# Block 3's down product and the last block's steps merged in one stage of a three-part kernel, with block 3's tokens turned by TensorE

## The chip, the cores and the metric

The kernel runs on one core of a Trainium2 chip. Its time is the device time of one launch in microseconds, the median of several launches. A profile is taken of one further execution. The engines are TensorE (PE; its weight loads are listed as PEld), VectorE (DVE), ScalarE (ACT), GpSimd (POOL) and SyncE (SP, which here only issues DMA transfers). Each executes its own queue in order.

## What is computed

Three layers, one behind the other, in fp32:

```python
q_p, k_p = phi(q * s), phi(k * s)               # 4 batches, 8 heads, 576 tokens, 128 features
x = (q_p @ (k_p.T @ v)) / (q_p @ k_p.sum(tokens) + 1e-6)      # linear attention -> 2304 x 512
gate = 1.0 / (1.0 + np.exp(-(x @ w_gate)))      # 512 -> 1536
x = gate * (x @ w_val) @ w_out                  # 1536 -> 512
logits = x @ phi                                # 512 -> 32 slots: 8 experts of 4
d = softmax(logits, over=tokens)
h = np.maximum((d.T @ x)[e] @ w1[e], 0.0)       # per expert e, 512 -> 1024
slot_out[e] = h @ w2[e]                         # 1024 -> 512
out = softmax(logits, over=slots) @ slot_out
```

## The kernel before

Tokens lie in five blocks: blocks 0 to 3 have 512 of them, the last one (block 4) has 256. In the gated layer a block goes through 12 steps, one for each 128 of the 1536 hidden features. A step has a gate product, a value product and a down product, which adds to four banks of PSUM. Every fp32 product is made of three passes: operands are split into a high part (`hi_of`, a copy that rounds) and the rest (`lo_of`, a subtraction), and `three` adds high x high, high x low and low x high. So a product of 128 features with one block has 12 matmuls (four groups of 128 rows, three passes each), of 512 columns, or of 256 for the last block.

Blocks 2 and 3 are a pair (`pair_jobs`). Their gate and value products are made together, by seven products instead of eight. Block 2's down product runs inside these steps; the hidden features of block 3 are kept in `GB` (fp32, in the region `g` and the pieces g1a and g1b), and block 3's down product follows as a stage of its own (`SPAND`, 33 us). Then come the last block's 12 steps (`moe_jobs`). Both load the same out weights, converted earlier and kept in DRAM (`wscr`, for each of the 12 f one gate, one value and one out part of 128x512), into the six slots of 128x512 of the ring `ws` (`WR`), and split them: for block 3 in `split_out`, for the last block in `split_w`.

The gate of a full block is a chain of Abs, Exp, Ln, a VectorE operation that reads the bank once more, and Exp. The last block's gate is one Sigmoid. Where a function follows on ScalarE that is in another set of tables than the one before it, its queue has an ACT_TABLE_LOAD ahead of it, which the compiler puts there.

When a block has left the gated layer (`evac_out`), the operations of the slot layer for its tokens follow (`moe2_chunks`): logits (`chunk_logits`), the running maximum and exp over tokens, tokens turned to token-major form, the turned exponentials (`chunk_ltT`, tile `lt`) times the turned tokens, added to `acc` (`chunk_slot`), and exp over slots (`cs`, `cT`). To turn the tokens of blocks 0 to 3, VectorE transposes 32x32 squares (`chunk_x2`, 4 operations of 128x512) and 16 DMA transfers of 64 KB on SP's queue (`chunk_back`, `x2T<-x`) bring the squares to their places. The last block's tokens are turned in `last_slots` by TensorE (product with `ident`) and two copies. `join_slots` brings `acc` to a common maximum. Then `last_slots`, `layer1` (8 experts, weights W1), `layer2` (weights W2) and `combine` end the program.

W1 (16.8 MB) is loaded by ScalarE's queue into regions of SBUF as they become free, W2 (32 pieces of 512 KB) by SP's queue into the regions that fall free towards the end (`free_more`, `free_halves`, `free_early`, `free_rest`).

The order on each engine isn't that of the code. Each job is given a due time (`jobs.append((time, stream, job))`), and each operation that it records is given to `Plan`, with a lead for its stream (`LEAD`). `Plan.schedule` then runs a model of the five engines with costs of its own (`cost`, `RELOAD` for a change of table) and puts the operations in an order for each engine; `Plan.issue` writes them out. So all instructions have one line of code, L425 (L432 in the changed kernel), and are told apart by their tiles: `ga`, `va`, `o0` to `o3`, `fl` (two buffers) are the eight banks of PSUM, written as `o` where numbers are left out; `w0`, `w1`, `w2` are the split weights of gate, value and out; `gt` the split hidden features, `XT4` the last block's input, `ga_a` the gate's scratch.

## Time and profile before

| | before |
|---|---|
| median of 3 runs | 669.89 us (667.93 to 673.65) |
| the profiled execution | 666.81 us, its span 664.9 us, mean granted clock 0.997 |
| busy: PE, DVE, ACT, POOL | 644.0, 479.7, 410.6, 289.2 us |
| block 3's down product | about 513.5 to 547 us of the span |
| the last block's 12 steps | about 547 to 611 us |
| last slots; layer 1; layer 2 | 611 to 618; 618 to 632.5; 632.5 to 655 us |

Times in the views are microseconds from the span's start. "Idle before" an instruction is the time its engine stood still ahead of it, with the engine and tile of the instruction that ended it (`[0.46 <-DVE w]`). Ends of matmuls are modelled, so a group's shown length is longer than the time from its start to the next one's start.

### The profile page before, as it was taken

Reading aid. Unit: us, or ns where it says so; the run is one execution under the profiler, and the core shown is the slowest. Engines: PE = TensorE matmul, PEld = TensorE weight load, DVE = VectorE, ACT = ScalarE, POOL = GpSimd, SP = SyncE. Lnnn points to the kernel's source line nnn. Section 1 sums busy time; section 2 is a strip of 40 time slices with the busy share of each in tenths; the row PEclk is TensorE's granted clock in tenths of the full one; section 3 lists DMA queues with packets and bytes.
Section 4 is the critical chain, followed back from the end, with each engine's and each line's share of the span. In section 5 each row is a group of like instructions: output and inputs, shape, how many; then the busy total and the mean of one; then the engine's idle time right before and its main releaser. Section 6 shows DMA issues by size and latency. Waiting matters only on the chain.

```text
span 664.9 us, 12634 instructions
## 1 busy us (share of the span) xinstructions
PE 644.0 (97%) x4268; PEld 513.2 (77%) x4268; DVE 479.7 (72%) x1379; ACT 410.6 (62%) x937; POOL 289.2 (43%) x272
## 2 busy tenths in 40 slices
PE   7899999999999999999999999999999999899995
PEld 5676777768888888888877778878888779899663
DVE  5898989888998765667689987557557757756323
ACT  4899989889998866777675654534442225445012
POOL 0456344455445344455453555555551453542100
PEclk9999999999999999999999999999999999999998
DMA  7987857678976345223315552222228899777988
GB/s 233 324 269 260 274 188 273 204 237 272 298 260 215 101 115 176 90 97 98 109 49 185 195 147 78 63 64 63 65 65 293 278 316 346 229 233 264 353 334 240
DMA packets 55216, 132.17 MB, mean 199 GB/s; under 512 B 6256, under 2 KB 14192, under 8 KB 55152
## 3 DMA queue, kind: packets, MB, share of 16 engines
q1 hardware_dynamic: 49328, 114.01, 52.7%
q10 hardware_dynamic: 5824, 17.37, 7.7%
q8 instruction: 33, 0.54, 0.3%
q14 instruction: 31, 0.25, 0.1%
HBM read 113.00 MB, written 14.16 MB: 191 GB/s over the span
## 4 chain that ended last, share of the span: by engine, by line
PE 84%; DMA 5%; DVE 4%; ACT 2%; POOL 1%; SPq 1%; issue 1%; DVEq 0%; POOLq 0%; ACTq 0%
PE o L425 24%; PE fl L425 23%; PE va L425 19%; PE ga L425 18%; DMA g<-in_tok 2%; DMA x2T<-x 1%; DMA g<-in_w 1%; DVE g L425 1%; DMA ws<-wscr 1%; SPq L425 1%; DVE XT L425 1%; POOL g L425 1%; DVE ga_a L425 1%; ACT w L425 0%; DMA g<-in_qkT 0%
## 5 line engine op out<-in xcount | busy, mean ns | idle before, releaser
L425 POOL TENSOR_TENSOR w<-ws,w 128x512 fp32r<-128x512 f32 (+1 forms) x101 | 120.6, 1195 | 161.3 <-ACT w L425 67.2
L425 PE MATMUL o<-gt,w 128*128 128x512 f32 (+1 forms) x576 | 134.7, 372 | 2.2 <-POOL w L425 0.9
L425 PEld LDWEIGHTS o<-gt,w 128*128 128x128 f32 x576 | 97.2, 189 | 24.4 <-issue 2.4
L425 PE MATMUL ga<-XT,w 128*128 128x512 f32 (+1 forms) x432 | 101.6, 367 | 0.9 <-POOL XT L425 0.9
L425 ACT ACTIVATE w<-ws 128x512 fp32r<-128x512 f32 (+1 forms) x100 | 57.7, 579 | 72.3 <-PE o L425 28.1
L425 PE MATMUL va<-XT,w 128*128 128x512 f32 (+1 forms) x432 | 100.1, 366 | 1.6 <-DVE ga_a L425 1.1
L425 PE MATMUL fl<-g,g 64*128 64x128 f32 (+4 forms) x686 | 84.1, 313 | 3.5 <-ACT g L425 1.7
L425 ACT ACTIVATE g<-g 128x128 f32<-128x128 f32 (+4 forms) x206 | 73.8, 414 | 16.9 <-DVE g L425 12.9
L425 PEld LDWEIGHTS ga<-XT,w 128*128 128x128 f32 x432 | 69.9, 189 | 16.8 <-issue 4.7
L425 PEld LDWEIGHTS va<-XT,w 128*128 128x128 f32 x432 | 70.5, 189 | 15.2 <-issue 2.4
L425 PEld LDWEIGHTS fl<-g,g 64*128 64x128 f32 (+2 forms) x686 | 60.3, 182 | 24.4 <-issue 7.3
L425 ACT ACTIVATE x2T<-g 128x512 f32<-128x512 f32 x72 | 45.8, 666 | 4.2 <-DVE x L425 2.4
L425 ACT ACTIVATE g1b<-g1b,g 128x128 f32<-128x128 f32 x128 | 40.8, 389 | 5.9 <-DVE g L425 5.7
L425 DVE TENSOR_SCALAR x2T<-x2T 128x512 f32<-128x512 f32 (+1 forms) x72 | 35.9, 513 | 3.7 <-ACT x2T L425 3.4
L425 POOL TENSOR_TENSOR g<-g 128x640 f32<-128x640 f32 (+1 forms) x19 | 23.4, 1230 | 33.3 <-DMA g<-in_tok 13.3
L425 DVE CUSTOM_DVE_ANT_0 g<-fl,g 128x128 f32<-128x128 f32 x142 | 32.3, 286 | 6.5 <-PE fl L425 6.4
L425 PE MATMUL o<-gt,ga_a 128*128 128x512 f32 x144 | 35.4, 393 | 0.0
L425 DVE TENSOR_TENSOR XT<-fl,XT 128x512 f32<-128x512 f32 x24 | 16.6, 690 | 23.0 <-PE fl L425 23.0
L425 POOL TENSOR_TENSOR x<-x2T 128x512 int32<-128x512 int32 x19 | 24.6, 1295 | 16.1 <-DVE x2T L425 11.3
L425 PEld LDWEIGHTS o<-gt,ga_a 128*128 128x128 f32 x144 | 26.7, 188 | 5.8 <-POOL ga_a L425 0.3
L425 ACT ACTIVATE ga_a<-ga_a 128x512 f32<-128x512 f32 x48 | 30.0, 624 | 1.7 <-DVE ga_a L425 1.4
L425 POOL TENSOR_TENSOR w<-x,w 128x512 fp32r<-128x512 f32 x15 | 19.3, 1285 | 24.2 <-DVE x2T L425 11.5
(254 smaller groups left out, 1264.3 us busy)
## 6 DMA issues: line engine op xcount, KB each, us to landing
ws<-wscr SPq DMA_DIRECT2D x42, 512.0 KB, 3.7
g<-in_wall SPq DMA_DIRECT2D x36, 512.0 KB, 5.0
ws<-wscr SPq DMA_DIRECT2D x54, 256.0 KB, 3.7
wscr<-x SPq DMA_DIRECT2D x36, 256.0 KB, 4.6
g<-in_qkT SPq DMA_DIRECT2D x15, 576.0 KB, 5.3
g<-in_tok SPq DMA_DIRECT2D x15, 576.0 KB, 5.1
g<-in_w ACTq DMA_DIRECT2D x16, 512.0 KB, 6.9
XT<-in_w ACTq DMA_DIRECT2D x12, 512.0 KB, 4.6
```

The source lines that it names most:

```text
L425: ins = getattr(self.eng[e], method)(*a, **k)
```

## The change

Block 3's down product and the last block's 12 steps are put into one stage, `tail_jobs`. In step f the out part is loaded and split once (`split_t(f, 2)`), and both blocks use it: `down_b` (block 3, 512 columns, banks ga, va, o0, o1) in step f and `down_c` (last block, 256 columns, banks o3 and fl) one step later. The last block's value and gate products share one bank, `o2`: the value in columns 256 to 511, the gate in 0 to 255. The ring has five slots; the sixth is the gate's scratch. The gates of f = 10 and 11 use Abs, Exp, Ln and Exp, with a `preload` of the table set that has Exp and Ln, and their value goes to bank ga. Block 3's tokens are turned by 16 TensorE products with `ident` and four copies (`turn_block`) in place of 4 VectorE transposes and 16 transfers. Its slot layer and the join fall at the end, from the last `down_b` on. W1's loads have other times (`W1S`), two pieces of the last expert's W1 are loaded in `last_slots`, and the regions for W2 fall free in another order.

```diff
     def load_part(k):
+
         if todo:
             m = todo.pop(0)
-            slot[USE[m]] = k
-            W[USE[m]] = WR[:, k, :]
-            SP.dma_start(out=W[USE[m]], in_=wscr[USE[m][0] % NF][:, USE[m][1], :])
+            f, p = USE[m]
+            slot[f, p] = k
+            SP.dma_start(out=WR[:, k, :], in_=wscr[f][:, p, :])
+        else:
+            spent.append(k)
+            if k < 4 and k ^ 1 in spent:
+                free_early(k & 2)
...
+    def split_t(f, part):
+
+        if part == 2:
+            t = OB[f % 3]
+        else:
+            t = T([128, 2, 512], f"w{part}", F32R)
+        w = WR[:, slot[f, part], :]
+        hi_of(t[:, 0, :], w, SITE["hw"])
+        lo_of(t[:, 1, :], w, t[:, 0, :], SITE["lw"])
+        WS[LAST + f, part] = t
+        if slot[f, part] < 5:
+            load_part(slot[f, part])
...
-        ps = bank(tag)[:, 0:n]
+        if i < LAST:
+            ps = bank(tag)[:, 0:n]
+        elif i < NS - 2:
+            if part == 1:
+                G["up"] = bank("o2")
+            ps = G["up"][:, n * part:n * part + n]
+        else:
+            ps = bank(("o2", "ga")[part])[:, 0:n]
...
         ps = up_passes(i, 0, "ga")
-        a = T([128, 512], "ga_a", F32, 2)[:, 0:n]
-        if i >= LAST:
+        a = WR[:, 5, n * (i % 2):n * (i % 2) + n] if i >= LAST else T([128, 512], "ga_a", F32, 2)[:, 0:n]
+        if LAST <= i < NS - 2:
             ACT.activation(out=a, in_=ps, func=AF.Sigmoid)
             return a
...
         lt = T([128, 2, 128], "lt", F32, 2)
+        if j == PAIR[1]:
+            plan.place([("ACT", "preload_act_table_set", (EXP_LN,), {})], [lt[0:p, 0, :], WR[:, 5, 0:256]], [WR[:, 5, 256:512]])
...
+    def turn_block(j, g):
+
+        x = ms[j]["x2T"]
+        ps = bank(("va", "o0", "o1", "va")[g])
+        for k in range(4):
+            PE.transpose(ps.rearrange("p (i k a) -> p k i a", i=4, k=4)[:, k], x[:, k, 128 * g:128 * g + 128], ident)
+        copy(ms[j]["y"][g], ps, (("ACT", "DVE"), ("DVE", "ACT"))[g % 2])
...
+        if j == PAIR[1]:
+            turns = [lambda g=g: turn_block(j, g) for g in range(4)]
+            return [lambda: chunk_logits(j)] + turns + [lambda: chunk_ltT(j), lambda: chunk_slot(j), lambda: chunk_cT(j)]
...
+        for s in range(NF + LAG + 1):
+            f = s - LAG
+            if s < NF:
+                add(t - 0.5, lambda s=s: split_t(s, 2))
+                add(t - 0.4, lambda s=s: late_split(s))
+            if s == NF - 1:
+                add(t, lambda: down_b(NF - 1, range(4)))
+                t += TAIL0
+                add(t, lambda: (evac_out(PAIR[1], banks[2]), turn_places()))
+                m2_jobs(PAIR[1], t + 0.2, M3, "m3")
+                add(t + 0.25 + M3, free_gt, "end")
+                add(t + 0.3 + M3, join_slots, "m3")
+            if f in (NF - 2, NF - 1):
+                add(t - 0.3, lambda f=f: split_t(f, 0))
+                add(t, lambda f=f: G.__setitem__("s", gate(LAST + f)))
+                add(t + 0.3, lambda f=f: split_t(f, 1))
+                t += TAIL1 / 3
+                add(t, lambda f=f: G.__setitem__("val", up_passes(LAST + f, 1, "")))
+                add(t + 0.01, lambda f=f: val(LAST + f, G.pop("s")))
+                t += TAIL1 / 3
+            elif 0 <= f < NF:
+                add(t - 0.3, lambda f=f: split_t(f, 1))
+                add(t, lambda f=f: G.__setitem__("val", up_passes(LAST + f, 1, "")))
+                add(t + 0.3, lambda f=f: split_t(f, 0))
+                t += TAIL1 / 3
+            if 0 <= f - 1:
+                add(t, lambda f=f: down_c(f - 1))
+                t += TAIL1 / 3
+                if f == NF - 1:
+                    add(t, free_more, "end")
+            if s < NF - 1:
+                add(t, lambda s=s: down_b(s, (0, 1)))
+                t += TAIL0 / 2
+            if 0 <= f < NF - 2:
+                add(t, lambda f=f: val(LAST + f, gate(LAST + f)))
+                t += TAIL1 / 3
+            if s < NF - 1:
+                add(t, lambda s=s: down_b(s, (2, 3)))
+                t += TAIL0 / 2
+        return t
```

The rows below are the orders that the planner wrote. First, PE in one step of the last block, before the change; block 3's down product is over by then. `fl_685<-ident_63,cs_671` turns block 2's slot weights.

```order
L425 MATMUL o3_659<-gt_643,w2_678 128x256 x3
L425 MATMUL ga_686<-XT4_106,w0_681 128x256 x12
L425 MATMUL va_689<-XT4_106,w1_683 128x256 x12
L425 MATMUL fl_685<-ident_63,cs_671 128x128
L425 MATMUL o0_656<-gt_643,w2_684 128x256 x2
```

And PE in one step after it, in the middle of the merged stage; the first row is the value product, the next two the last block's down product of the step before, and `w2_587` and `more_586` are split out parts.

```order
L432 MATMUL o2_629<-XT4_106,w1_628 128x256 x12
L432 MATMUL o3_609<-gt_591,more_586 128x256
L432 MATMUL fl_610<-gt_591,more_586 128x256
L432 MATMUL o3_609<-gt_591,more_586 128x256 x5
L432 MATMUL fl_610<-gt_591,more_586 128x256 x5
L432 MATMUL ga_592<-gt_588,more_586 128x512 x3
L432 MATMUL va_593<-gt_588,more_586 128x512 x3
L432 MATMUL o2_629<-XT4_106,w0_630 128x256 x12
L432 MATMUL o0_594<-gt_588,more_586 128x512 x3
L432 MATMUL o1_595<-gt_588,more_586 128x512 x3
L432 MATMUL o2_633<-XT4_106,w1_632 128x256 x12
```

Value and gate were in banks of their own, with 12 matmuls of the down product behind them; now they share `o2`, and six matmuls of 512 columns stand between the gate and the next step's value.

Second, ScalarE from the last sigmoid of the last block on, before the change: the last gate is `ga_a_732`, the join's exp is `mx2_721`.

```order
L425 ACTIVATE ga_a_718<-ga_717 128x256
L425 ACTIVATE w1_727<-ws_85 128x512
L425 ACTIVATE w2_728<-ws_85 128x512
L425 ACT_TABLE_LOAD
L425 ACTIVATE mx2_721<-mrun_72,mx2_721 128x1
L425 ACT_TABLE_LOAD
L425 ACTIVATE ga_a_732<-ga_731 128x256
L425 ACTIVATE x2T_729<-o1_657 128x256
```

And after it, from the last sigmoid's successor on: `gt_647` and `ga_a_648` are turned groups of block 3's tokens, `ws_85` is the gate's scratch, `o2_650` gate 10's bank and `o2_665` gate 11's, `lt_652` the exponentials of block 3's logits.

```order
L432 ACTIVATE gt_647<-va_655 128x512
L432 ACTIVATE ga_a_648<-o1_658 128x512
L432 ACT_TABLE_LOAD
L432 ACTIVATE mx2_653<-mrun_72,mx2_653 128x1
L432 ACTIVATE ws_85<-o2_650 128x256
L432 ACTIVATE ws_85<-ws_85 128x256
L432 ACT_TABLE_LOAD
L432 ACTIVATE ws_85<-ws_85,one_b_64 128x256
L432 ACT_TABLE_LOAD
L432 ACTIVATE ws_85<-ws_85 128x256
L432 ACT_TABLE_LOAD
L432 ACTIVATE lt_652,mx2_653<-fl_651,mx2_653 128x128
```

Four loads of a table stand within twelve rows; the last of them is the preload, behind the functions of gate 10.

Third, PE in the closing stretch of the changed kernel, from gate 10 on: `lt_652` is turned by `fl_661`, and `dt_662` is the turned tile.

```order
L432 MATMUL o2_650<-XT4_106,w0_646 128x256 x12
L432 MATMUL va_659<-ident_63,g1a_506 128x4x32 x4
L432 MATMUL ga_656<-XT4_106,w1_654 128x256 x12
L432 MATMUL o3_609<-gt_591,more_586 128x256 x6
L432 MATMUL fl_610<-gt_591,more_586 128x256 x6
L432 MATMUL o2_665<-XT4_106,w0_660 128x256 x9
L432 MATMUL fl_661<-ident_63,lt_652 128x128 x2
L432 MATMUL o2_665<-XT4_106,w0_660 128x256 x3
L432 MATMUL ga_669<-XT4_106,w1_666 128x256 x7
L432 MATMUL fl_667<-gt_647,dt_662 32x512 x2
```

Gate 11's twelve matmuls are in two parts, and the turning of `lt` stands between them; before, the only foreign rows in the last two steps were the join's.

## Rows read from the trace of the kernel before

**Rows 1.** The page: busy time of the engines, share of the span, instructions.
```profile
PE 644.0 (97%) x4268; PEld 513.2 (77%) x4268; DVE 479.7 (72%) x1379; ACT 410.6 (62%) x937; POOL 289.2 (43%) x272
```

**Rows 2.** Busy time by stretches: stretch, length, each engine (instructions), granted clock, DMA share, GB/s.
```profile
513.50:546.00 32.50, 31.96 (x167) 25.15 (x167) 23.52 (x47) 8.42 (x15) 16.27 (x12) 1.00 0.91 301
585.00:611.00 26.00, 26.00 (x217) 24.86 (x216) 16.46 (x39) 10.99 (x18) 10.63 (x8) 1.00 0.67 217
513.50:611.00 97.50, 94.44 (x673) 82.79 (x673) 66.10 (x138) 38.83 (x65) 44.62 (x33) 1.00 0.84 274
```

**Rows 3.** Instructions in time (start, us, engine, operation): PE at full rate.
```profile
549.26 2.91 PE L425 MATMUL o<-gt,ga_a 128*128 128x512 f32 x12
552.01 1.59 PE L425 MATMUL va<-XT,w 128*128 128x256 f32 x12
...
585.68 1.60 PE L425 MATMUL ga<-XT,w 128*128 128x256 f32 x12
```

**Rows 4.** Instructions in time, PE: where matmuls are missing.
```profile
537.34 0.61 PE L425 MATMUL o<-gt,w 128*128 128x512 f32 x2
...
538.41 2.56 PE L425 MATMUL o<-gt,w 128*128 128x512 f32 x10 [0.46 <-DVE w L425]
...
574.13 1.60 PE L425 MATMUL ga<-XT,w 128*128 128x256 f32 x12
...
576.79 0.50 PE L425 MATMUL va<-XT,w 128*128 128x256 f32 x2 [1.06 <-DVE ga_a L425]
```

**Rows 5.** Instructions in time, SP's queue and ScalarE: what those gaps wait for.
```profile
572.94 2.42 SPq L425 DMA_DIRECT2D x2T<-x  x3
...
577.40 0.63 ACT L425 ACTIVATE w<-ws 128x512 fp32r<-128x512 f32 x1 [5.91 <-DMA ws<-wscr]
```

**Rows 6.** Groups of instructions by shape, 513.5 to 611 us: busy, mean ns, idle before.
```profile
L425 POOL TENSOR_TENSOR w<-ws,w 128x512 fp32r<-128x512 f32 x27 | 35.5, 1315 | 54.1 <-ACT w L425 32.1 <-DVE w L425 10.7 <-DVE gt L425 5.6
...
L425 ACT ACTIVATE w<-ws 128x512 fp32r<-128x512 f32 x30 | 18.8, 631 | 41.6 <-DMA ws<-wscr 13.4 <-PE o L425 9.9 <-PE va L425 6.6
...
L425 ACT ACT_TABLE_LOAD x8 | 10.3, 1283 | 1.5 <-PE o L425 1.3
```

**Rows 7.** DMA issues, 513.5 to 611 us: size, median us to landing.
```profile
ws<-wscr SPq DMA_DIRECT2D x36, 256.0 KB, 3.9
```

**Rows 8.** Instructions in time, PE: transposes of the last block's tokens.
```profile
613.64 0.66 PE L425 MATMUL fl<-ident,x2T 128*128 128x128 f32 x4
```

**Rows 9.** Instructions in time: from gate product to sigmoid; a multiplication.
```profile
587.12 1.60 PE L425 MATMUL va<-XT,w 128*128 128x256 f32 x12
...
587.33 0.38 ACT L425 ACTIVATE ga_a<-ga 128x256 f32<-128x256 f32 x1 [0.76 <-DVE w L425]
...
608.32 0.42 DVE L425 TENSOR_TENSOR ga_a<-va,ga_a 128x256 f32<-128x256 f32 x1 [0.32 <-ACT ga_a L425]
```

**Rows 10.** Instructions in time: the join, and the last exponential's product.
```profile
606.29 0.29 ACT L425 ACTIVATE mx<-mrun,mx 128x1 f32<-128x1 f32 x1
...
607.44 0.23 DVE L425 TENSOR_SCALAR dt<-srep,mx 128x32 f32<-128x32 f32 x1
...
607.73 0.97 PEld L425 LDWEIGHTS fl<-dt,acc 128*128 128x128 f32 x8 [0.17 <-DVE dt L425]
...
615.34 1.86 PEld L425 LDWEIGHTS o<-dt,x 128*128 128x128 f32 x16 [0.34 <-ACT dt L425]
```

**Rows 11.** Instructions in time, ScalarE: around one table load.
```profile
564.54 0.63 ACT L425 ACTIVATE w<-ws 128x512 fp32r<-128x512 f32 x1 [0.59 <-issue]
...
565.19 1.28 ACT L425 ACT_TABLE_LOAD   x1
...
566.49 0.39 ACT L425 ACTIVATE ga_a<-ga 128x256 f32<-128x256 f32 x1
```

**Rows 12.** Instructions in time, PE: opening of the paired stage.
```profile
361.93 0.47 PE L425 MATMUL o<-gt,w 128*128 128x512 f32 x1 [0.76 <-ACT XT L425]
```

**Rows 13.** Instructions in time, SP's queue: the last transfers of W2.
```profile
633.31 2.21 SPq L425 DMA_DIRECT2D g<-in_w  x2
```

More of the change, by code (lines that the diff above doesn't have):

```diff
@@ L64 @@
 FLOOR = 8
-WIDE = 15
 SQP = [0, 0, 1, 1, 1, 0, 1, 0]
@@ L80 @@
 SPAND = 33.0
+LAG = 1
+M3 = 6.0
+M2 = 45.0
+W1S = [1.0, 8.0, 15.0, 22.0, 24.0, 36.0, 50.0, 63.0, 29.0]
+W2S = 2.0
+TAIL0, TAIL1 = 2.75, 4.2
 READY = 12.0
@@ L395, in schedule @@
                     c, held = self.cost(e, alt[1], alt[3], outs, ins)
-                    want = {AF.Exp: 0, AF.Ln: 0, AF.Sigmoid: 1}.get(alt[3].get("func"), table) if e == "ACT" else table
+                    want = 0 if alt[1].startswith("preload") else {AF.Exp: 0, AF.Ln: 0, AF.Sigmoid: 1}.get(alt[3].get("func"), table) if e == "ACT" else table
                     if want != table:
@@ L761, in body @@
     cw = {}
-    USE = [(i + (p < 2), p) for i in range(LAST - 1, NS) for p in range(3) if LAST <= i + (p < 2) < NS]
+    USE = [(f, p) for s in range(NF + LAG) for f, p in ((s, 2), (s - LAG, 1), (s - LAG, 0)) if 0 <= f < NF and (p < 2 or f > 1)]
     slot, todo = {}, list(range(len(USE)))
@@ L1122, in pieces, with load_w1 @@
         return [t[:, 1024 * c:1024 * c + 1024] for c in range(n)]
-    def load_w1():
-        e = len(W1)
-        if e < E:
-            W1.append(pieces(EXTAGS[e], 3 if EXTAGS[e] == "XT" else 1))
-            for c in range(4):
-                ACT.dma_start(out=W1[e][c], in_=w1[e, :, 1024 * c:1024 * c + 1024])
+    def load_w1(x=None, cs=range(4)):
+        if x is None:
+            e = len(W1)
+            x = pieces(EXTAGS[e], 3 if EXTAGS[e] == "XT" else 1)
+            W1.append(x)
+        e = next(k for k, y in enumerate(W1) if y is x)
+        for c in cs:
+            ACT.dma_start(out=x[c], in_=w1[e, :, 1024 * c:1024 * c + 1024])
     def load_w2():
@@ L1263, in layer1 @@
         ps = bank(("ga", "va")[e % 2])[:, 0:256]
-        for k in range(4):
+        order = (2, 3, 0, 1) if e == E - 1 else range(4)
+        for n, k in enumerate(order):
             for g in range(4):
                 PE.matmul(ps[32 * g:32 * g + 32, :], si[:, k, :], W1[e][k][:, 256 * g:256 * g + 256],
-                          start=k == 0, stop=k == 3)
+                          start=n == 0, stop=n == 3)
         if e == 0:
@@ L1514, in pair_jobs, with tail_jobs, buffers, late_split @@
-        add(t + SPAND - 6.0, lambda: (split_w(LAST, 0), split_w(LAST, 1)))
-        return t + SPAND
-    def m2_jobs(j, t, span):
+        return t + SPANQ
+    OB = []
+    def tail_jobs(t):
+        add = lambda at, f, name="moe": jobs.append((at, name, f))
+        def buffers():
+            m = T([128, 2, 2, 512], "more", F32R)
+            OB.extend([m[:, 0], m[:, 1], T([128, 2, 512], "w2", F32R)])
+            slot.update({(0, 2): 4, (1, 2): 5})
+            y = T([128, 2, 512], "gt", F32R, 2)
+            x = [T([128, 512], "ga_a", F32R, 2) for _ in range(2)]
+            G["late"] = (y[:, 0], y[:, 1]), x
+            ms["x2T"], ms["x2"] = G["h"], G["h"][:, 1024:2048].rearrange("p (g c) -> p g c", g=2)
+            G["last"] = T([128, 2, 2, 256], "gt", F32R, 2)
+        def late_split(f):
+            gt = G["late"][f % 2]
+            hi_of(gt[0], GB[f], SITE["hg"])
+            lo_of(gt[1], GB[f], gt[0], SITE["lg"])
+        def down_b(f, ks):
+            if f == 0 and ks[0] == 0:
+                banks[2] = [bank(x) for x in ("ga", "va", "o0", "o1")]
+            w, g = WS[LAST + f, 2], G["late"][f % 2]
+            for k in ks:
+                c = slice(128 * k, 128 * k + 128)
+                three(banks[2][k], (w[:, 0, c], w[:, 1, c]), g, f == 0, f == NF - 1)
+        def down_c(f):
+            if f == 0:
+                banks[1] = [bank("o3"), bank("fl")]
+            w, g = WS.pop((LAST + f, 2)), G.pop(LAST + f)
+            for k in range(4):
+                c = slice(128 * k, 128 * k + 128)
+                ps = banks[1][k // 2][:, 256 * (k % 2):256 * (k % 2) + 256]
+                three(ps, (w[:, 0, c], w[:, 1, c]), (g[:, 0, 0:256], g[:, 1, 0:256]),
+                      f == 0 and k % 2 == 0, f == NF - 1, True)
+        def turn_places():
+            y = T([128, 2, 512], "gt", F32, 2)
+            G["y"] = y
+            ms[PAIR[1]]["y"] = [y[:, 0], y[:, 1]] + [T([128, 512], "ga_a", F32, 2) for _ in range(2)]
+        add(t - 0.6, buffers)
+        add(t - 0.50 * SPANQ / 6, lambda: (load_part(0), load_part(1)))
+        add(t - 0.1 * SPANQ / 6, lambda: (load_part(2), load_part(3)))
+        for s in range(NF + LAG + 1):
[38 more added lines that the diff above has]
+        return t
@@ L1518, in m2_jobs @@
+    def m2_jobs(j, t, span, name="m2"):
         m2c = moe2_chunks(j)
-        jobs.extend((t + span * k / len(m2c), "m2", c) for k, c in enumerate(m2c))
+        jobs.extend((t + span * k / len(m2c), name, c) for k, c in enumerate(m2c))
     xt(1)
```

94 lines of the change are left out of this document (38 added, 56 removed).

## The prediction

> **What bounds the kernel now.** I read the page first. PE is busy for 644.0 us, 97% of the span [rows 1]; no other engine comes near. TensorE's granted clock is 1.00, its level of 2.4 GHz, in every stretch of the tail that I read [rows 2]. So a change can win only three things: matmul work, idle time between matmuls, or the two ends of the program. The second view, busy time by stretches, says how much idle there is where the change works. From 513.5 to 611 us (block 3's down product and the last block's 12 steps) PE is busy 94.44 of 97.50 us; from 585 on there is none left [rows 2]. The third view, the order of instructions in time on PE, says where it lies. At full rate twelve 128x512 matmuls take 2.75 us from start to start and twelve of 128x256 take 1.44 [rows 3]; a group's own length is shown some 0.16 us longer, since ends are modelled. The gaps are few: two matmuls at 537.34 are followed only at 538.41, 1.07 us later where 0.46 would do (0.61 missing), and the gate product of 574.13 only at 576.79 (2.66 less 1.44, 1.22 missing) [rows 4]. I find seven such places from 537 to 585. Each hides a modelled end of some 0.17 us, so the idle time of the busy-time view, 97.50 - 94.44 = 3.06 us, stands for 3.06 + 7 x 0.17 = 4.25 us of missing matmul time.
>
> The fourth view is what those gaps wait for. PE names VectorE or GpSimd, but the cause is behind them. ScalarE stood 5.91 us until a load `ws<-wscr` had landed, and on SP's queue three copies of turned tokens, `x2T<-x`, took 2.42 us to be issued just before [rows 5]. The out, gate and value weights of the last block come late because they queue behind block 3's turned tokens, and before that share the wires with W1 (DMA share 0.91) [rows 2].
>
> **The matmul work doesn't change.** Block 3's down product keeps its 144 matmuls of 128x512 (33.0 us), the last block its 432 of 128x256 (51.8 us). Sharing the split of the out weights takes away 12 hi copies (0.63 us on ScalarE), 12 lo subtractions (1.32 on GpSimd) [rows 6] and 12 loads of 256 KB [rows 7]. ScalarE, VectorE and GpSimd are busy 38.8, 66.1 and 44.6 of 97.5 us [rows 2], so this is worth nothing by itself, only what late splits cost.
>
> **Term 1, the gaps go: -4.25 us.** Sixteen copies `x2T<-x` leave SP's queue, and the out loads halve, so the loads that were late (36 of 256 KB, 3.9 us to landing in the median [rows 7]) have more time. In the new order a step has 1.44 + 1.44 + 1.38 + 1.44 + 1.38 = 7.08 us of matmuls, with three splits in it instead of three in 4.3 us. Bounds: 0 to -4.25; I take all of it, and put what returns in term 3.
>
> **Term 2, tokens turned on PE: +1.9 us.** The 16 transposes are 128x128 as in the existing `fl<-ident,x2T`: four are shown with 0.66 us [rows 8], 0.49 without the modelled end of 0.17, 0.12 each: 16 x 0.12 = 1.9 us on the engine that sets the end. What is taken away for it, 4 stream transposes on VectorE, lay beside PE. Bounds 1.0 (by 0.06 each, a quarter of a 128x512 matmul's 0.23) and 2.6 (by the group's whole 0.66). The evacuations are in term 4.
>
> **Term 3, what is late in the new steps: +1.0 us.** Two things. Value and gate of a step now share one bank, `o2`. The next value product can't start before the sigmoid and the product have read the gate: 0.21 us from the last gate matmul (587.12, where the next product starts) to the sigmoid, 0.38 for it, 0.42 for the multiplication [rows 9], and two hand-overs of 0.06, as from VectorE's `dt` (done at 607.67) to PE at 607.73 [rows 10]: 1.13 us. Six matmuls of block 3's second half lie between, 1.38 us: cover enough by 0.25 us. It is gone where a 0.63 us split of ScalarE [rows 6] starts just ahead of the sigmoid: at most 0.38 a step. And the ring of five slots gives a load 11.8 us from one use of a slot to the next (5 pieces at 3 per 7.08 us), some 8 us when hi, lo and the lead are taken off. In the first steps block 2's 16 copies `x2T<-x` still stand between these loads on SP's queue, and W1 is under way; the same mixture of loads gave the 0.61 us at 537.3 [rows 4]. Bounds: 0, and 3.8 for ten steps of 0.38. I take 1.0, nearer to zero, since the engines beside PE are at most 68% busy in the stretch today (66.1 of 97.5) [rows 2] and lose work.
>
> **Term 4, the closing stretch: +3.7 us.** Before, the closing of the last block had 0.17 us of PE idle, for the join (`dt` to `fl<-dt,acc`) [rows 10]. Now everything of block 3's tokens (logits, turns, exponentials, slots, join) falls in the last two steps, and these two gates go by Abs, Exp, Ln, Exp. In ScalarE's order the preload of the set that has both stands behind gate 10's functions, not ahead of them. So four table loads, 1.28 us each [rows 6], stand in one chain: ahead of the maximum's exp, of Ln, of the last Exp and of the logits' exp. I set the clock to zero at the last matmul of block 3's down product and work it out with 0.63 for a copy of 128x512 [rows 6], 0.38 for a function of 128x256 [rows 9] and 0.29 for the maximum's exp [rows 10]. ScalarE evacuates until 0.8, copies two turned groups (to 2.5, the second waits for PE), loads a table (3.8), does the maximum's exp (4.1), Abs and Exp of gate 10 (4.9; its product ended at 3.3), loads (6.2), Ln (6.6), loads (7.9), Exp (8.3), loads (9.6), exp of the logits (10.0). PE has its own work to 6.6; gate 11 then waits until VectorE has read gate 10's bank behind Ln (7.2): 0.6. Nine matmuls later the two transposes of `lt` stand in PE's order ahead of gate 11's last three matmuls. PE is there at 8.3 and waits till 10.05: 1.8. Behind that, gate 11's own chain of five functions, the join's exp and three VectorE operations end about 1.3 us after PE's cover (value and down step of f=10, 1.44 each, and the slots' products). Sum 0.6 + 1.8 + 1.3 = 3.7. Bounds: 0 (if PE's cover is longer than I count) and 5.6 (should the four evacuations all lie ahead of it, 3 x 0.63 more).
>
> The trace shows no more than the load's own time: a split ends at 565.17, the load starts at 565.19, the sigmoid at 566.49 [rows 11]. The Trainium skill ("ScalarE: Activation LUTs", What ACT_TABLE_LOAD costs) adds about 1.38 us of drain to each switch, 2.66 in all. By it the three loads more than one preload would cost 4.1 us more; the rows above disagree. The same page (Table sets: the hidden batching unit) says that one set holds both exp and ln and that one load then does. It is what this kernel asks for; the four loads in its order are what the rule speaks against.
>
> **Terms 5 and 6, small: -0.85 us.** The exp of the last slots waits for a load now: 0.34 us of PE idle ahead of `o<-dt,x` [rows 10]; after the change that set is loaded already: -0.35. In the opening of the paired stage PE idles 0.76 us for a ScalarE copy [rows 12], and the same planner reorders operations there: -0.5 (bounds +0.5 and -0.76). W2's transfers start 1 to 3 us later at most. Their last two are issued from 633.3 to 635.5 [rows 13] while PE has products of the second layer to about 655 (span 664.9 less its end of some 10 us): cover of over 10 us even if they take 5, so nothing; without it each us late would count in full.
>
> **Sum.** -4.25 + 1.9 + 1.0 + 3.7 - 0.35 - 0.5 = +1.5 us. The profiled execution took 666.81 us, below all three others (667.93, 669.89, 673.65); by it the new time is 668.3. The mean of the four is 669.6, and I forecast on that scale: 669.6 + 1.5 = 671.1 us.
>
> **The rivals.**
> (a) The closing is hidden: PE's own work there covers ScalarE's chain, term 4 is 0: 671.1 - 3.7 = 667.4. For it: before, only 0.17 was seen there [rows 10]. Against it: PE has some 8 us of work ahead of the point and the chain is 10 long. It decides at whether the exp of the logits is done before PE reaches gate 11's ninth matmul.
> (b) Slower: the shared bank. If in each of ten steps a split or a late load holds ScalarE or VectorE back by 0.95 us behind the gate's end, 0.95 - 0.25 = 0.7 a step is lost: +7.0 - 1.0 (term 3) = +6.0, 677.1. For it: a cast for the next gate's weights stands on VectorE ahead of the multiplication and waits for its load, and DMA is 0.91 busy where W1 loads [rows 2]. Against it: the ring's 8 us against 3.9 to landing [rows 7]. It costs from 0.25 us of lateness on, and decides from 0.92 (0.67 lost a step).
> (c) Each of the three loads more than one preload holds ScalarE as long again as the load itself, since in this chain each comes straight behind a function whose result it must let out: 3 x 1.28 = +3.8, 674.9. For it: before, such pairs were not on the path. Against it: 0.02 us between end and start on either side of a load [rows 11]. The drain that the Trainium skill (ScalarE: Activation LUTs, What ACT_TABLE_LOAD costs) tells of would look like this.
> (d) Faster than any of this: all gaps of the opening go too and term 3 and 4 are zero: -4.25 + 1.9 - 0.35 - 0.76 = -3.5, 666.1. To be 1% faster it would have to find 3 us more, for which no gap is left in the tail.
>
> **Chances.** Forecast, 668.5 to 674: 0.52. (a) 0.20, (b) 0.14, (c) 0.07, (d) 0.07. A measurement of this kernel can tell about 1%, 6.7 us, from no change. Faster by more than that: half of (d), 0.04. Slower: most of (b) and a part of (c), 0.11. Within 1%: 0.85. The range that leaves 2 in 10 out runs from (d)'s and (a)'s lower part (666 less one), 665, to (b)'s 677.
>
> **What would show it.** Term 1: no PE gap over 0.3 us between the start of the merged stage and its last down step, and ScalarE waits under 2 us for `ws<-wscr`. Term 2: 16 transposes `<-ident` of 0.12 us on PE. Term 3: idle of the value product put down to VectorE's multiplication. Term 4: four table loads within 10 us, and PE waiting 1 to 2 us for `lt` in the middle of gate 11. The forecast is wrong if the loads are elsewhere, if PE waits in each step for bank `o2`, or if the stretch before the tail moves by over 1 us.

## The result, and the profile after

The changed kernel is slower by a little: 674.40 us against 668.59 us (medians of 15 runs each), ratio 1.0087 with an interval of 1.0068 to 1.0106, or 5.8 us. The forecast was +1.5 us (671.1 us), with a range of 665 to 677 and a chance of 0.85 for a change of less than 1%.

| | before | after |
|---|---|---|
| median of 15 runs | 668.59 (665.38 to 673.65) | 674.40 (671.09 to 677.28) |
| the profiled execution | 666.81, span 664.9 | 677.28, span 675.5 |
| mean granted clock | 0.997 | 0.986 |
| first product of the paired stage starts | 357.33 | 359.30 |
| last product of the paired stage to first of layer 1 ("the tail") | 109.9 | 118.7 |
| first product of layer 1 to the end of the span | 46.9 | 47.0 |

The profiled execution of after is the slowest of its 15 and that of before is below its median, so the two traces differ by 10.5 us where the medians differ by 5.8. About 2 us of that are in the attention at the start; over the twelve profiles of this study the paired stage begins between 355.9 and 359.6 us, before and after alike. The paired stage takes 0.4 us less, the end of the program 0.1 us more, and the tail, where the change is, 8.9 us more. So the tail is read below.

The page of after, busy time of the engines (answers [rows 1]):

```profile
PE 649.9 (96%) x4284; PEld 518.1 (77%) x4284; DVE 471.0 (70%) x1368; ACT 410.1 (61%) x936; POOL 282.6 (42%) x269
```

PE does 16 instructions more and is busy for 5.9 us longer, though 16 transposes of 0.11 us are only 1.8. The view of busy time by stretches of after (stretch, length, each engine's busy time, granted clock, DMA share, GB/s; it answers [rows 2]) tells where the time is lost and what the clock did:

```profile
513.50:541.50 28.00, 28.00 (x198) 24.78 (x196) 20.46 (x41) 14.12 (x20) 9.03 (x7) 1.00 0.89 276
541.50:546.00 4.50, 2.76 (x20) 2.21 (x19) 3.55 (x7) 0.00 (x0) 1.38 (x2) 1.00 0.91 292
...
549.00:557.00 8.00, 4.88 (x27) 4.35 (x26) 3.17 (x6) 0.63 (x1) 2.56 (x2) 0.82 0.95 334
557.00:600.00 43.00, 43.00 (x289) 38.11 (x288) 22.89 (x41) 9.83 (x18) 15.51 (x12) 0.99 0.53 167
...
609.00:616.50 7.50, 5.58 (x31) 4.14 (x32) 2.76 (x12) 4.97 (x10) 0.95 (x2) 0.77 0.42 140
```

PE stands still in three places, but for some 0.3 us in small pieces. It is idle 1.74 of 4.5 us behind 541.5, 3.12 of 8 us behind 549 and 1.92 of 7.5 us behind 609 (and 0.4 us just ahead of 609), and the last two of these have a lower granted clock, 0.82 and 0.77. From 557 to 600, which before had gaps of its own, nothing is missing.

Who ended those waits is told by the view of waits (engine, who was waited for, us in total, times, longest), for PE in the tail of after:

```profile
PE o L432 <- DVE ws L432: 5.4, 3, 3.1
PE fl L432 <- ACT lt L432: 1.7, 1, 1.7
```

`ws` on VectorE is the operation that reads bank `o2` for the last time: the multiplication with the gate's scratch in the first two waits, the operation behind gate 10's Ln in the third. PE waited for it to get the bank back. `lt` on ScalarE is the exponential of block 3's logits.

The first gap, in order of time, on SP's queue, VectorE and PE of after (answers [rows 4, 5]):

```profile
532.73 5.29 SPq L432 DMA_DIRECT2D x2T<-x  x8
...
538.12 1.97 SPq L432 DMA_DIRECT2D ws<-wscr  x3
...
542.20 0.43 DVE L432 CAST w<-ws 128x512 fp32r<-128x512 f32 x1 [2.00 <-DMA ws<-wscr]
...
543.14 0.42 DVE L432 TENSOR_TENSOR ws<-o,ws 128x256 f32<-128x256 f32 x1
...
543.61 1.70 PE L432 MATMUL o<-XT,w 128*128 128x256 f32 x12 [1.74 <-DVE ws L432]
```

Eight transfers of block 2's turned tokens (`x2T<-x`) take 5.29 us on SP's queue. Three weight loads (`ws<-wscr`) are issued only at 538.12. VectorE's cast of the next gate's weights waits for one of them until 542.20, the multiplication stands behind the cast, and the value product gets its bank at 543.61, 1.74 us late. The second gap (the chain that ended last has the load in it):

```profile
542.36 9.41 DMA ws<-wscr
```

```profile
540.90 0.81 SPq L432 DMA_DIRECT2D x<-in_w  x2
...
551.12 0.34 ACTq L432 DMA_DIRECT2D XT<-in_w  x1
551.89 0.43 DVE L432 CAST w<-ws 128x512 fp32r<-128x512 f32 x1 [3.58 <-DMA ws<-wscr]
552.23 0.42 DVE L432 TENSOR_TENSOR ws<-o,ws 128x256 f32<-128x256 f32 x1
...
552.70 1.88 PE L432 MATMUL o<-XT,w 128*128 128x256 f32 x12 [3.12 <-DVE ws L432]
```

The same pattern: cast at 551.89 behind a load that took 9.41 us to land, multiplication at 552.23, value product at 552.70, 3.12 us late. That product then takes 1.88 us as shown where 1.60 is usual [rows 3].

The closing, ScalarE and PE of after (answers [rows 9 to 11]):

```profile
604.57 1.28 ACT L432 ACT_TABLE_LOAD   x1
...
606.89 1.28 ACT L432 ACT_TABLE_LOAD   x1
...
608.19 0.51 ACT L432 ACTIVATE ws<-ws,one_b 128x256 f32<-128x256 f32 x1
608.72 1.28 ACT L432 ACT_TABLE_LOAD   x1
608.73 0.42 DVE L432 SCALAR_TENSOR_TENSOR ws<-o,ws 128x256 f32<-128x256 f32 x1 [0.91 <-ACT ws L432]
...
609.21 1.33 PE L432 MATMUL o<-XT,w 128*128 128x256 f32 x9 [0.58 <-DVE ws L432]
...
610.01 0.42 ACT L432 ACTIVATE ws<-ws 128x256 f32<-128x256 f32 x1
610.45 1.28 ACT L432 ACT_TABLE_LOAD   x1
...
611.74 0.37 ACT L432 ACTIVATE lt<-fl,mx 128x128 f32<-128x128 f32 x1
...
612.25 0.69 PE L432 MATMUL fl<-ident,lt 128*128 128x128 f32 x2 [1.71 <-ACT lt L432]
...
613.38 1.70 PE L432 MATMUL ga<-XT,w 128*128 128x256 f32 x7
...
615.01 0.85 PE L432 MATMUL fl<-gt,dt 128*32 128x512 f32 x2
```

There are four table loads within 7.2 us. Gate 11 (`o<-XT,w`, nine matmuls) waits 0.58 us: VectorE reads gate 10's bank at 608.73, behind Ln (608.19), and Ln stands behind the second load. The turning of `lt` waits 1.71 us behind the last load, the preload. The seven matmuls at 613.38 then take 1.63 us to the start of the next product, at 615.01, where seven times 0.12 [rows 3], 0.84, would do.

### The profile page after: what moved, and what is told of

Same layout as the page of the kernel before. It is cut to its first block, busy times and chain, and to the rows that moved or that the text cites. A ratio compares the mean times of both kernels' runs of the same rounds, so it can differ in the third digit from the quotient of the medians.

```text
span 675.5 us, 12556 instructions
## 1 busy us (share of the span) xinstructions
PE 649.9 (96%) x4284; PEld 518.1 (77%) x4284; DVE 471.0 (70%) x1368; ACT 410.1 (61%) x936; POOL 282.6 (42%) x269
## 4 chain that ended last, share of the span: by engine, by line
PE 87%; DMA 4%; DVE 4%; ACT 2%; SPq 1%; issue 1%; POOL 1%; DVEq 0%; POOLq 0%; ACTq 0%
PE o L432 26%; PE fl L432 25%; PE va L432 18%; PE ga L432 17%; DMA ws<-wscr 1%; DVE g L432 1%; SPq L432 1%; DMA g<-in_w 1%; DVE XT L432 1%; ACT L432 1%; DMA g<-in_von 1%; DVE ga_a L432 1%; POOL g L432 1%; DMA x2T<-x 1%; DVE w L432 0%
## 5 line engine op out<-in xcount | busy, mean ns | idle before, releaser
L432 PE MATMUL o<-gt,w 128*128 128x512 f32 (+1 forms) x396 | 103.0, 394 | 0.8 <-ACT XT L432 0.8
L432 PE MATMUL ga<-XT,w 128*128 128x512 f32 (+1 forms) x312 | 86.4, 403 | 1.7 <-POOL XT L432 1.7
L432 PEld LDWEIGHTS o<-gt,w 128*128 128x128 f32 x396 | 71.2, 188 | 19.3 <-issue 2.2
L432 ACT ACTIVATE w<-ws 128x512 fp32r<-128x512 f32 (+1 forms) x83 | 47.0, 566 | 56.6 <-PE o L432 19.9
L432 PE MATMUL va<-XT,w 128*128 128x512 f32 x288 | 80.1, 406 | 0.0
L432 PEld LDWEIGHTS ga<-XT,w 128*128 128x128 f32 x312 | 55.6, 191 | 17.4 <-issue 4.5
L432 PEld LDWEIGHTS va<-XT,w 128*128 128x128 f32 x288 | 52.3, 188 | 12.1 <-issue 2.2
L432 PE MATMUL o<-XT,w 128*128 128x256 f32 x264 | 36.3, 287 | 5.4 <-DVE ws L432 5.4
L432 PEld LDWEIGHTS o<-XT,w 128*128 128x128 f32 x264 | 34.6, 193 | 7.8 <-DVE ws L432 6.5
L432 DVE CAST w<-ws 128x512 fp32r<-128x512 f32 x29 | 12.4, 426 | 31.0 <-PE o L432 16.7
```

Of the source, the lines that this page charges most:

```text
L432: ins = getattr(self.eng[e], method)(*a, **k)
```

## The experiments

All ratios are to the kernel before, run beside each group of experiments (its medians there are 668.6 to 669.4 us), so a ratio is not the median of a row over 668.59. Differences in microseconds are differences of ratios times 668.6; with the intervals of both they are good to some 2.5 us either way (4 for e4). "Tail" is as in the table above, from the one profile of each: 109.9 us before, 118.7 after.

| kernel | median us | ratio (95% interval) | tail us |
|---|---|---|---|
| after | 674.40 | 1.0087 (1.0068 to 1.0106) | 118.7 |
| e1: table load ahead of gate 10 | 671.49 | 1.0029 (0.9996 to 1.0062) | 113.7 |
| e2: block 2's transfers left out | 667.90 | 0.9969 (0.9947 to 0.9991) | 111.6 |
| e3: W2's pieces due later | 674.01 | 1.0067 (1.0034 to 1.0100) | 116.1 |
| e4: multiplication ahead of the cast | 677.79 | 1.0112 (1.0054 to 1.0170) | 121.5 |
| e5: block 2's transfers on ScalarE's queue | 669.92 | 1.0012 (0.9984 to 1.0040) | 111.7 |
| e6: W2's pieces held back | 672.24 | 1.0054 (1.0025 to 1.0084) | 118.5 |
| e7: e5 and e1 | 666.60 | 0.9966 (0.9938 to 0.9994) | 107.9 |
| e8: block 2 turned by TensorE, and e1 | 666.16 | 0.9963 (0.9939 to 0.9986) | 109.9 |
| e9: before, transfers on ScalarE's queue | 668.55 | 1.0008 (0.9980 to 1.0037) | 110.9 |
| e10: W1's loads spread | 673.16 | 1.0066 (1.0038 to 1.0095) | 115.9 |

### e1: the table load ahead of gate 10

```diff
-            plan.place([("ACT", "preload_act_table_set", (EXP_LN,), {})], [lt[0:p, 0, :], WR[:, 5, 0:256]], [WR[:, 5, 256:512]])
...
-                add(t, lambda: (evac_out(PAIR[1], banks[2]), turn_places()))
+                add(t, lambda: (plan.place([("ACT", "preload_act_table_set", (EXP_LN,), {})], [WR[:, 5, 0:256]], [WR[:, 5, 256:512]]),
+                                evac_out(PAIR[1], banks[2]), turn_places()))
```

> The changed kernel with the load of the table set that has exp and ln placed ahead of gate 10's functions, right behind the last sigmoid, instead of behind them; ScalarE's order then has one table load in the closing, not four. Nothing ahead of the closing changes. Theory (the loads stand in the chain): the 0.58 us before gate 11 and the 1.71 us before the turning of lt go, and with them the slow clock that follows (granted 0.77 from 609 to 616.5): PE idle in the closing falls from 2.6 us to under 0.8, the kernel is about 3 us faster than the changed one, ratio to before 1.004 to 1.005. Rival (evacuations and VectorE's steps set the end, the loads are covered by them): the waits come back for another operation and the time is within 0.7 us of the changed kernel, 1.008 to 1.0095.

Measured: 1.0029, 3.9 us less than after. ScalarE of e1 has one load, at 592.79, and the exponential of the logits comes at 600.46, ahead of gate 10's functions:

```profile
592.79 1.28 ACT L432 ACT_TABLE_LOAD   x1
...
600.46 0.36 ACT L432 ACTIVATE lt<-fl,mx 128x128 f32<-128x128 f32 x1
...
601.40 0.38 ACT L432 ACTIVATE ws<-o 128x256 f32<-128x256 f32 x1 [0.30 <-PE o L432]
...
601.63 0.38 PE L432 MATMUL fl<-ident,lt 128*128 128x128 f32 x2
```

Busy time by stretches of e1, the closing without its last 11 us:

```profile
513.50:596.00 82.50, 78.11 (x535) 69.49 (x533) 48.08 (x92) 24.64 (x39) 29.10 (x23) 0.98 0.71 225
596.00:608.50 12.50, 12.50 (x113) 10.12 (x114) 6.82 (x28) 6.87 (x17) 2.58 (x2) 1.00 0.31 111
```

PE is busy all of the 12.5 us with the clock at 1.00, while the 4.4 us ahead of them that wait for the bank stay. So the loads were in the chain, and were worth 3.9 us: the two waits (2.3 us), and the low clock that went with them. One thing is not separated: with the load gone the planner also put the turning of `lt` ahead of gate 11 and the join's products elsewhere.

### e2: block 2's transfers left out

```diff
-        back = [lambda h=h: chunk_back(j, h) for h in range(4)]
+        back = [lambda h=h: chunk_back(j, h) for h in range(4)] if j != PAIR[0] else [lambda: None] * 4
```

> The changed kernel without the 16 transfers that bring block 2's turned tokens to their places (left out; block 2 goes into the slots unturned). Theory (a weight load that stands behind them on SP's queue is late, VectorE's cast waits for it, and the value product waits behind the cast): the gap of 1.9 us at 541.5 goes; that of 3.3 at 549.2, whose load is issued later, behind two transfers of W2, stays or halves. 2 us faster than the changed kernel, ratio to before 1.005 to 1.006. Rival (the shared bank alone, whatever the loads do): both gaps stay, 1.008 to 1.009.

Measured: 0.9969, 7.9 us less than after, four times what was expected. Both gaps went, also the second, which I had put down to W2:

```profile
513.50:598.00 84.50, 84.50 (x609) 74.86 (x609) 51.61 (x103) 28.69 (x47) 30.25 (x24) 1.00 0.64 219
598.00:619.00 21.00, 18.43 (x138) 15.29 (x137) 9.92 (x37) 9.13 (x19) 2.13 (x3) 0.92 0.62 231
```

The waits of the closing stay, in the second row. As the bytes of the transfers are gone too, this run doesn't tell their traffic from their place on the queue; e5 does.

### e3 and e6: W2's two pieces later

```diff
-W2S = 2.0
+W2S = 17.0
...
         free.extend(pieces("x2T", 1, 2) + pieces("x2", 1, 2))
+        plan.floor = plan.t
         load_w2()
+        plan.floor = 0.0
```

In e3 only the first line was changed, and it moved nothing: the two transfers were still issued at 539.78, at the same place of SP's order. So e3 is the changed kernel once more (ratio 1.0067), and shows how far a repetition goes: its gaps in the same two places are 0.29 and 3.40 us, where after has 1.74 and 3.12, and its tail is 2.6 us shorter.

> The changed kernel with the two transfers of W2 into the regions of block 2's tokens (512 KB each, issued on SP's queue at 540.9 just ahead of the weight loads) 15 us later. Theory (these two, with W1's pieces of the same moment, are what makes the next weight loads take 9.4 us): the gap of 3.3 us at 549.2 goes or falls under 1 us, that of 1.9 at 541.5 stays: 2.5 to 3 us faster than the changed kernel, ratio 1.004 to 1.005. Rival (W1's traffic alone sets the landing): loads still take 8 us and more, gap over 2 us, ratio 1.007 to 1.009.

e6 has the floor as well, and there the two pieces are issued behind eight further weight loads.

> The changed kernel with W2's two pieces into block 2's regions held back in the order until 8 weight loads later (in the run before this the due time alone was moved and the transfers stayed where they were). Theory A (these 1 MB with W1's 1 MB of the same moment make the loads land after 9 us): the gap of 3.3 us falls under 1.5, that of 1.9 stays; 2 us faster than the changed kernel, ratio 1.005 to 1.006. Theory B (the loads are issued too late already, since block 2's transfers stand ahead of them; the bunch of W1 is enough): the second gap stays over 2.5 us, ratio 1.007 to 1.009.

Measured: 1.0054, tail 118.5 where after has 118.7. VectorE and PE of e6:

```profile
530.09 5.39 SPq L432 DMA_DIRECT2D x2T<-x  x8
...
543.17 0.43 DVE L432 CAST w<-ws 128x512 fp32r<-128x512 f32 x1 [5.03 <-DMA ws<-wscr]
...
544.59 0.80 PE L432 MATMUL o<-XT,w 128*128 128x256 f32 x2 [4.78 <-DVE ws L432]
```

The second gap is gone, and the first has grown to 4.78 us. Four of W1's pieces (`XT<-in_w`) came forward into the room that W2 had left: they are issued from 533.3 to 539.8 us, in after from 540.7 to 551.1. That they delayed the load of this cast fits, but was not tested. The ratio is in theory A's range, the gaps are those of neither theory. Their sum, some 5 us, is that of after; so W2's pieces bear on where the wait falls, and holding them back did not make it shorter.

### e4: the multiplication ahead of the cast

```diff
-        hi_of(t[:, 0, :], w, SITE["hw"])
+        if part == 0 and 0 < f < NF - 1:
+            n = 256 * ((LAST + f - 1) % 2)
+            plan.place([("DVE", "tensor_copy", (), {"out": t[:, 0, :], "in_": w})], [t[:, 0, :]], [w, WR[:, 5, n:n + 256]])
+        else:
+            hi_of(t[:, 0, :], w, SITE["hw"])
```

> The changed kernel with VectorE's multiplication of a step ordered ahead of the cast of the next gate's weights (the cast is made to depend on the multiplication), loads as they are. Theory (the cast that waits for its load holds the multiplication behind it, and so the shared bank and the value product): the value product no longer waits; the gate alone waits for its own weights, 4.3 us later in PE's order less 1.7 for the split: the two gaps of 1.9 and 3.3 us fall to 0 to 1 us together, 4 us faster than the changed kernel, ratio 1.002 to 1.004. Rival (the loads are so late that the gate itself waits as long): the same gaps stand before the gate product instead of the value product, ratio 1.007 to 1.009.

Measured: 1.0112, with a tail some 2.7 us longer than after's; the intervals of the two ratios overlap. The edit changed more than it should: with it the planner put 11 of block 2's transfers in a row on SP's queue, and the product of block 2's slots came to stand early on PE:

```profile
525.52 9.86 SPq L432 DMA_DIRECT2D x2T<-x  x11
...
540.86 1.88 PE L432 MATMUL fl<-x2T,dt 128*32 128x512 f32 x2 [7.00 <-DMA ws<-wscr]
```

PE waits 7.00 us at that product, which needs block 2's turned tokens; the last of their transfers lands at 540.45. Whether the order of cast and multiplication alone would have saved the gaps is not settled by this run; what it shows is a third wait behind the same transfers.

### e5: block 2's transfers on another queue

```diff
-            SP.dma_start(out=x[32 * h:32 * h + 32, 512 * i:512 * i + 512], in_=y[32 * i:32 * i + 32, h])
+            (ACT if j == PAIR[0] else SP).dma_start(out=x[32 * h:32 * h + 32, 512 * i:512 * i + 512], in_=y[32 * i:32 * i + 32, h])
```

> The changed kernel with block 2's 16 transfers of turned tokens issued by ScalarE's queue instead of SP's; they still run, with the same bytes. Theory (it is the place on SP's queue, ahead of the weight loads, that hurts): both gaps (1.9 and 3.3 us) go as when the transfers were left out, 5 to 6 us faster than the changed kernel, ratio to before 0.996 to 0.998. Rival (the transfers themselves crowd the wires, 8 us of them with W1): the loads still land late, a gap of over 2 us stays, ratio 1.002 to 1.007; or ScalarE, waiting for a transpose ahead of a transfer, holds its splits and the sigmoid, gaps of 1 us before value products.

Measured: 1.0012, 5.0 us less than after, and a tail of 111.7 us against 111.6 with the transfers left out.

```profile
513.50:602.00 88.50, 88.27 (x622) 77.10 (x621) 53.65 (x109) 27.04 (x46) 29.66 (x23) 1.00 0.70 228
602.00:621.00 19.00, 16.43 (x133) 13.59 (x132) 9.46 (x37) 8.62 (x19) 2.01 (x2) 1.00 0.70 258
```

PE is idle 0.23 us in 88.5 up to the closing. From 520 to 556 us the DMA engines are no less busy than in after (share 0.95 against 0.90): the 16 transfers are issued in the same stretch (521 to 545 us), beside 12 pieces of W1, where after has 10. (W2's two pieces fall later in e5, at 556.5; but e2 has no gaps with them at 521 to 525, and in e6, which holds them back too, the gaps stay.) So neither the bytes of the transfers nor W1's traffic is the cause; the place of the transfers ahead of the weight loads on SP's queue is. The gain is the 5 us that was expected, from which a ratio of 1.000 to 1.001 follows; the ratios expected, 0.996 to 0.998, were reckoned too low. (Its ratio is 0.4% above that of e2, though their tails are alike; the intervals overlap.)

### e10: W1's loads spread

```diff
-W1S = [1.0, 8.0, 15.0, 22.0, 24.0, 36.0, 50.0, 63.0, 29.0]
+W1S = [1.0, 12.0, 24.0, 34.0, 40.0, 46.0, 54.0, 63.0, 50.0]
```

> The changed kernel with W1's loads spread over the merged stage (due 1, 12, 24, 34, 40 to 54 us after its start instead of 1, 8, 15, 22, 24, 36), block 2's transfers on SP's queue as they are. Rival to the queue (W1's traffic is what makes the weight loads late): weight loads land within 4 us, both gaps of 1.9 and 3.3 us go, 5 us faster than the changed kernel, ratio 1.000 to 1.002. Queue theory: loads land sooner (4 to 5 us instead of up to 9), so the second gap goes, but the first, whose load waits to be issued, stays at 1 to 2 us: 3 us faster, ratio 1.003 to 1.005.

Measured: 1.0066, above the ranges of both theories. Both gaps stay, 1.61 and 1.95 us:

```profile
542.74 1.69 PE L432 MATMUL o<-XT,w 128*128 128x256 f32 x12 [1.61 <-DVE ws L432]
...
550.46 1.71 PE L432 MATMUL o<-XT,w 128*128 128x256 f32 x12 [1.95 <-DVE ws L432]
```

The other due times did not thin out W1 where the gaps are: from 520 to 556 us ten of its pieces are issued in both kernels, the DMA engines move 285 GB/s here and 287 in after, and a weight load lands after 5.4 us in the median (after: 5.0). So this run doesn't test W1's traffic; e5 does. The second gap is 1.2 us shorter than in after; between after and e3, which have the same order on SP's queue, the first gap differs by more.

### e7 and e8: both mendings

e7 has the edits of e1 and e5. In e8 block 2's tokens are turned by TensorE as block 3's are, with no transfer left:

```diff
+        if j == PAIR[0]:
+            turns = [lambda g=g: turn_two(j, g) for g in range(4)]
+            return [lambda: chunk_logits(j)] + turns + [lambda: chunk_ltT(j), lambda: chunk_cT(j), lambda: chunk_slot(j)]
...
+        x, ps = ms[j]["x2T"], bank()
+        for k in range(4):
+            PE.transpose(ps.rearrange("p (i k a) -> p k i a", i=4, k=4)[:, k], x[:, k, 128 * g:128 * g + 128], ident)
+        copy(ms[j]["y"][g], ps, (("ACT", "DVE"), ("DVE", "ACT"))[g % 2])
```

> Both mendings: block 2's transfers on ScalarE's queue, and the table load ahead of gate 10. Theory (two separate places, additive): 5.5 us and 3 to 5 us less than the changed kernel, 8.5 to 10 in all, ratio to before 0.991 to 0.994; PE idle from the first step of the merged stage to the last slots under 1 us. Rival (the one gives back what the other gains, since W1's or W2's loads become the bound at the end): ratio 0.996 to 1.0, with waits of layer 1 or layer 2 for in_w.

> As the kernel with both mendings, but block 2's tokens are turned by TensorE too (16 products with ident and four copies), so that no transfer of turned tokens is left in the tail. Theory: the 16 products cost 16 x 0.11 = 1.8 us of PE against the version with the transfers on ScalarE's queue, ratio 0.994 to 0.997. Rival (ScalarE's queue still delays W1 or splits in the other version, and is free here): same or faster than it, 0.990 to 0.993.

Measured: 0.9966 and 0.9963. Both are faster than before, by 0.3% (intervals below 1), and than after by 1.2%. The stretches of e7:

```profile
513.50:592.00 78.50, 78.48 (x542) 69.45 (x540) 49.48 (x97) 21.35 (x35) 28.52 (x23) 1.00 0.74 247
592.00:605.00 13.00, 13.00 (x119) 10.84 (x119) 7.00 (x29) 7.41 (x18) 2.58 (x2) 1.00 0.32 105
```

There is no gap and no slow clock up to 605 us. The two mendings add up within the scatter: by the ratios 0.9966 against 1.0087 is 8.1 us, where e1 gave 3.9 and e5 5.0. The expected 0.991 to 0.994 was missed, and the ratio of e7 lies in the range of its rival. But what the rival said, a bound in the layers behind, is not there: from the first product of layer 1 to the end e7 takes 47.1 us, before 46.9 and after 47.0. The tails of e8 and e7 differ by 2.1 us, the price of 16 transposes and what they push, while their times don't differ beyond the intervals.

### e9: the same remedy in the kernel before

```diff
-            SP.dma_start(out=x[32 * h:32 * h + 32, 512 * i:512 * i + 512], in_=y[32 * i:32 * i + 32, h])
+            (ACT if j in PAIR else SP).dma_start(out=x[32 * h:32 * h + 32, 512 * i:512 * i + 512], in_=y[32 * i:32 * i + 32, h])
```

> The kernel before, not merged, with the 32 transfers of turned tokens of blocks 2 and 3 on ScalarE's queue instead of SP's. Theory (the 4.25 us of gaps before the change came from the same place on SP's queue): most of them go without any merging, 3 to 4 us faster than before, ratio 0.994 to 0.9955. Rival (the gaps come from six ring slots and short steps of 4.3 us, or ScalarE's queue now holds splits and W1 behind transposes): 0.997 to 1.001.

Measured: 1.0008, no change. The gaps from 571 to 585 are gone, but ScalarE now stands behind its own transfers, and PE behind ScalarE:

```profile
540.92 0.63 ACT L425 ACTIVATE ga_a<-ws 128x512 fp32r<-128x512 f32 x1 [5.81 <-DMA x2T<-x]
```

```profile
541.60 4.84 PE L425 MATMUL o<-gt,ga_a 128*128 128x512 f32 x12 [2.48 <-ACT ga_a L425]
```

The rival held here. So moving the transfers alone doesn't give what e7 gives. Between the first and the last of block 2's transfers on its queue ScalarE has four splits here (520.3 to 540.3 us), in e7 none (519.3 to 541.3). In e7, too, a split behind them waits 4.9 us (at 543.21), but PE has other work; why it is covered there was not tested.

## Why the prediction was right, and where it was off

The time, 674.4, is in the range, and it moved by less than 1%, as forecast. Of the 5.8 us the sum had 1.5. That the time is still in the range is in part luck: it lies 0.4 us above the band of the forecast itself (668.5 to 674), the scale of 669.6 was 1.0 us above the later median of before, and the upper end of the range was rival (b)'s, whose loss in each step did not come. By its number the time is nearest to rival (c), 674.9, which fell. The sign "the stretch before the tail moves by over 1 us" can't be read from one profile, since its start varies by 3.7 us over the twelve.

**What bounds the kernel.** Right: PE, and its few gaps. [rows 2] gave the measure in which everything could be counted.

**Term 1, the gaps go (-4.25).** Right for the second half of the stage: where the last block alone ran before, the merged stage has no gap (557 to 600: 43.00 of 43.00). Its own sign, no gap over 0.3 us from the start of the merged stage on, was not met by after; it was met by e7. Counted from start to start before had six such places, not seven, from 537 to 585, and 4.0 us missing, not 4.25.

**Term 2, 16 transposes (+1.9).** Right. In after five of them in a row take 0.71 us with the modelled end:

```profile
603.20 0.71 PE L432 MATMUL o<-ident,g1a 128*128 128x128 f32 x5
```

Without 0.17 that is 0.54, 0.11 each, 1.8 us.

**Term 3, what is late in the new steps (+1.0).** This is the term that was mis-sized. The place and the chain were those that it and rival (b) named: a weight load behind block 2's transfers on SP's queue, the cast on VectorE that waits for it, the multiplication behind the cast, the shared bank. But PE lost 1.74 and 3.12 us idle there, and with the slow clock behind them e5 puts the price at 5.0 us, e2 at 7.9. My bound of 3.8 was reckoned as ten steps of 0.38 us, a split of 0.63 less the cover of 0.25; what happened were two waits as long as a load is late. The mistake was to take the price of such mixing from one gap of before, 0.61 us [rows 4], and the loads' window from the median of 3.9 us to landing [rows 7], when the load that counted stood behind 5.3 us of transfers on SP's queue and another took 9.41 us to land. Rival (b)'s form, a loss in each step, did not happen: from 557 on the cover of 1.38 us was enough.

**Term 4, the closing (+3.7).** Right in mechanism and nearly in size. Gate 11 waited 0.58 (0.6 forecast) and the turning of `lt` 1.71 us (1.8). The third piece, 1.3 us behind gate 11's functions, was not there as a wait (0.16 us ahead of one weight load), but PE ran slowly in the same 7.5 us. The whole is worth 3.9 us by e1. Rival (a), that it is hidden, fell.

**Rival (c), a load that costs as much again.** Fell. In the closing of after the load at 608.72 ends at 610.00 and Exp starts at 610.01; a function ends at 608.70 and this load starts at 608.72. The Trainium skill's drain of about 1.38 us for each switch ("ScalarE: Activation LUTs", What ACT_TABLE_LOAD costs) does not show in these rows. The rule of the Trainium skill ("ScalarE: Activation LUTs", Table sets: the hidden batching unit) that one load does for exp and ln is what e1 follows, and e1's ScalarE needs no further load through both gates.

**Terms 5 and 6 (-0.85).** The wait ahead of `o<-dt,x` is gone, as forecast:

```profile
625.80 1.97 PE L432 MATMUL o<-dt,g1a 128*128 128x32 f32 x16
```

The paired stage is 0.4 us shorter, which is near the 0.5 forecast by luck: the gap that I named is still there with 0.77 us instead of 0.76 [rows 12]:

```profile
363.89 1.16 PE L432 MATMUL o<-gt,w 128*128 128x512 f32 x4 [0.77 <-ACT XT L432]
```

By the tails of the profiles, with each matmul's time to the next one's start less what is usual for its shape, the account is: transposes +1.8, gaps +3.8 (8.2 against 4.4), matmuls that ran at the lower clock about +3.1, small others +0.2: 8.9 us. The sum had -4.25 + 1.9 + 1.0 + 3.7 - 0.35 = +2.0 for the same stretch. Of the 6.9 us between, about 4.2 are term 3's two gaps (5.2 instead of 1.0) and 3.1 the clock, which the sum did not have; term 4's two waits, 2.6 instead of 3.7, take 1.1 off, and small terms add 0.7. The 15 runs say that the tail of this one execution is at the long side of what is usual; how the 5.8 us of the medians divide among the terms is known only from e1, e2 and e5.

## What to carry to other kernels

Before merging two stages, write down what else stands on the queues that feed them, in the order in which it is issued: a stage whose own transfers have been removed can still stand behind those of the stage before it. An operation that waits for a load makes one chain with an operation behind it that gives a buffer back, as in both gaps here; whether the other order would have helped, e4 did not show. And a preload of a table belongs ahead of the first function of its set: behind gate 10's functions it was a fourth load, ahead of them (e1) it was the only one.
